# Moving the value load, cutting the filler products, and giving 345 planned steps their own due times in an attention and two-MLP kernel

## The chip, the core and the metric

One NeuronCore of a Trainium2 chip runs the kernel. The metric is the device time of one execution in microseconds (us). Engines are named as in the profile: PE is the matrix engine TensorE, DVE is VectorE, ACT is ScalarE, POOL is GpSimd, SP is the engine whose queue issues most of the DMAs. TensorE has two clock levels here, 1.2 and 2.4 GHz; a granted clock of 1.00 in the profile is the upper one.

## The reference

Attention with a mask by blocks of 64 positions, its heads joined to a matrix of 2304 tokens by 512, then two MLPs with 2048 hidden features:

```python
batch, n_heads, seq, head_dim = (4, 8, 576, 64)
scores = scale * np.matmul(q, k.transpose(0, 1, 3, 2))
scores = np.where(block_i >= block_j, scores, -1000000000.0)
attn = np.exp(scores - np.max(scores, axis=-1, keepdims=True))
attn = attn / (np.sum(attn, axis=-1, keepdims=True) + 1e-09)
x = np.matmul(attn, v)                       # to (2304, 512)
r = np.maximum(x @ w_in, 0.0)
x = (s * (r * r) + b) @ w_out                # first MLP
h = x @ w2_in
out = np.maximum(0.01 * h, h) @ w2_out       # second MLP
```

## The kernel before

The tokens are cut into five blocks (NB = 5) by position in the sequence: block k holds positions 128k to 128k+127 of all four batches, 512 tokens (the last block 256). Block 0 is the first tile. Its attention has to be finished before the first MLP can start on it. After that, the MLP of one block (16 chunks f of 128 hidden features) and the attention of the next block run side by side, so that PE always has products to do while DVE and ACT work on the softmax. The second MLP follows in six sections; it uses the seven-product scheme of Strassen and Winograd on 2 by 2 blocks.

The first tile is done in four pairs of heads (p = 0 to 3). For each pair the loads of keys (fk, L653) and queries (fq, L659) are issued, for the first three pairs half by SP and half by ACT, for the fourth all six by SP. Then come the scores (L597), the row maxima (L558), the exponentials (L567), the normalisation (L582), the transposes through PE (t, L612) with their copies out of PSUM (L528 on ACT, L530 on DVE), the product with the values (o, L700; the values of all four pairs are one load of 1 MB, fv, L666), and the split of the result into a high and a low part (xh on ACT, L708; xl on DVE, L710). Scores are laid into PSUM banks y0 to y3, outputs and every second transpose into the two banks of s.

The weights of the first MLP arrive as words of 8 bytes and are decoded chunk by chunk in block 0 (tile early): DVE shifts (L365), ACT scales (L368), DVE joins (L371), ACT takes the high part (L384), DVE takes the low part (L387). A chunk then gives the h products (m_in, L929, 12 groups of one 128x512 product), a ReLU on ACT (L945), a square on ACT or DVE (L943), a high part (L947), a low part (L948) and the y products (m_out, L972). There is one PSUM bank for h in these blocks, so the h products of a chunk wait until the ReLU and the square of the chunk before have read the bank.

To keep PE from idling ahead of that, the program issues products of a zero tile with itself (warm, L634): WARM = 8 of 128 columns and FILL = 26 of 256 columns. Each is seen as two PE instructions in the trace. The 26 have a due time of 60, later than any work of the first tile, so that the planner gives them to PE only when nothing else is ready.

The order of all instructions is made when the program is built. Graph.add collects 4516 steps, each with its engine, its estimated cost, the steps it follows, the buffers it opens and a due time. Graph.order then plays a list schedule: whenever an engine is free, it takes from the steps that are ready by the planner's clock the one with the smallest due time, and writes it next in that engine's program. On the chip each engine keeps that order, whatever the real times are. DMA steps are planned with s.wire (time on the DMA engines), s.land (time to the landing) and at most eight out at once (LANES).

Of the kernel before, what the change touches and what calls it, by code (L numbers as in the profile page):

```python
# [43 lines left out]
class Graph:  # L44
# [11 lines left out]
    def add(self, eng, fn, after=(), opens=(), uses=(), due=0.0, port=False, nbytes=0, rel=0.0, mode="f", behind=(), run=2048, tail=0.0):  # L56
# [4 lines left out]
        s.tail = tail  # L61
        s.wire = nbytes / abs(run) * (12.0 + abs(run) / 23.0) / 16e3
        s.land = 1.5 if run > 0 else 0.5
        for p in s.preds:
# [29 lines left out]
    def order(self):  # L94
# [3 lines left out]
        events, n, out_there = [], 0, 0  # L98
        port, dma, mode = None, 0.0, "f"
        out = []  # L100
        turn = {}
        for i, s in enumerate(self.steps):
            s.rank = (s.due, i)
            for b in s.opens:
                if b.key in self.inturn:
                    turn.setdefault(b.key, []).append(s)
            if not s.left:
                heapq.heappush(events, (s.rel, n, "ready", s, None))
                n += 1
        for k in turn:  # L110
            turn[k].sort(key=lambda s: s.rank, reverse=True)
        while events:
# [27 lines left out]
            for e in idle:  # L140
# [42 lines left out]
                if s.nbytes:  # L183
                    dma = max(dma, end + 1.0) + s.wire
                    end = dma + s.land
                    out_there += 1
# [18 lines left out]
def act(n, ptr=0, acc=False):  # L205
    return 0.205 + n / 1195 + 0.125 * acc


def dve(n, rate=1):
    return 0.155 + n / 960 / rate  # L210
# [8 lines left out]


NB = 5
ORDER = (0, 1, 2, 4, 3)
# [3 lines left out]
def kernel(  # L226
# [23 lines left out]
    scale = 1.0 / float(D) ** 0.5  # L250
    FILL = 26
    WARM, LATE, PACE, AHEAD = 8, 10, (6.0, 4.9), 3
# [145 lines left out]
    def first_weights():  # L398
        for f in range(NF):
# [9 lines left out]
            if f < 1:  # L409
                chunk(w, raw, f, [lds[0]], [0], due)  # L410
                a = chunk(w, raw, f, [lds[1]], [1], due + 2)
            else:
                a = chunk(w, raw, f, lds, [0, 1], due)
            if f < KEEP or f >= NF - KEEP:
                slot = f if f < KEEP else f - NF + 2 * KEEP
                kept_ok[f] = G.add(
                    {"SP": 0.65}, lambda e, w=w, slot=slot: e.dma_start(out=kept[slot], in_=w().bitcast(F32).rearrange("p a n -> p (a n)")),
                    [a], [], [w], due + 8, run=-8192, nbytes=1048576)

# [121 lines left out]
    def softmax(k, banks, cols, P, pcols, due, after):  # L541
# [11 lines left out]
        for j, bk, c, n, r in groups:  # L553
            def fn(e, j=j, bk=bk, c=c, n=n, r=r):
                i = bk()[:, c:c + n * r]
                if r > 1:
                    i = i.rearrange("p (r n) -> p r n", r=r)
                e.reduce_max(out=nm()[:, j:j + r], in_=i, axis=AX.X)  # L558
            mx.append(G.add({"DVE": dve(n * r)}, fn, [after[j + r - 1]], [nm] * (j == 0), [nm, bk], due - 4))
        neg = G.add(  # L560
# [4 lines left out]
        for j, (bk, c, n) in enumerate(cols):  # L565
            def fn(e, j=j, bk=bk, c=c, n=n):
# [3 lines left out]
                )  # L570
            ex.append(G.add({"ACT": act(n, 1, True)}, fn, [neg], [l] if j == 0 else [], [P, l, nm, bk], due - 3.5))
        a = G.add(
# [74 lines left out]
    for p in range(NP):  # L647
# [16 lines left out]
        if p == 0:  # L664
            id_ok = G.add({"SP": 0.65}, lambda e: e.dma_start(out=id_sb, in_=ident), due=-39.5, run=512, nbytes=65536)
            fv_ok = G.add({"SP": 0.65}, lambda e: e.dma_start(out=fv(), in_=v[:, :128].rearrange("b s d -> s b d")), [], [fv], due=-37.5, run=2048, nbytes=1048576)  # L666
            sb_ok = [
# [11 lines left out]
    for p in range(NP):  # L679
        due = 10.0 + 4.0 * p  # L680
        y0, y1 = [bank(key, "s") for key in (("y0", "y1"), ("y2", "y3"), ("y0", "y1"), ("y2", "y3"))[p]]
# [50 lines left out]
    def later_block(blk):  # L732
# [8 lines left out]
        for u in range(NP * B):  # L741
# [48 lines left out]
            if flat:  # L790
# [16 lines left out]
                for h in range(2):  # L807
# [5 lines left out]
                        out=P()[:, nk * h:nk * h + nk], in_=bk[h]()[:, :nk], func=ACTF.Exp, bias=nm()[:, h:h + 1], scale=1.0,  # L813
                        accum_out=l()[:, h:h + 1]), mx, [P, l] * (h == 0), [P, l, nm, bk[h]], due - 3.5)
                    for h in range(2)
# [15 lines left out]
            else:  # L831
# [6 lines left out]
                for j in range(2):  # L838
# [8 lines left out]
                    for j in range(2)  # L847
# [5 lines left out]
                        out=P()[:, half * j:half * j + half], in_=bk[j]()[:, :half], func=ACTF.Exp, bias=nm()[:, 0:1], scale=1.0,  # L853
                        accum_out=l()[:, j:j + 1]), [neg], [l] * (j == 0), [P, l, nm, bk[j]], due - 3.5)
                    for j in range(2)
# [351 lines left out]
    def out_phase(n):  # L1207
# [13 lines left out]
        for o, r in enumerate(IN_ORDER):  # L1221
            z, first = where[r]
            for i in range(4):
                due = t2[n] + 28 * ONE + (4 * o + i) * ONE if o > 1 else t2[n] + (7 * min(i + 2, 4) + 2 * (i + o / 2) + 1 * (i == 3)) * ONE
# [28 lines left out]
                after = [hi, lo, out_ok[n, r], *[ev.get(({6: 1, 7: 6, 4: 7, 3: 5}.get(r), d)) for d in range(2)]]  # L1253
                p = G.add({"PE": ONE}, fn, after, z if first and i == 0 else [], [*z, gh, gl, out_w[n, r]], due)
            for d in range(2):
# [3 lines left out]
                if fresh:  # L1259
                    a = G.add({"ACT": act(NH)}, lambda e, y=y, z=z, d=d: copy(e, y()[:, d], z[d]()[:, :NH]), [p], [y] if y.opener is None else [], [y, z[d]], due + ONE)  # L1260
                else:
                    a = G.add({"DVE": dve(NH)}, lambda e, y=y, z=z, d=d: add(e, y()[:, d], z[d]()[:, :NH]), [p, prev], [], [y, z[d]], due + ONE)
                ev[r, d] = ye[j, to[r], d] = a
# [82 lines left out]
```

## Time and profile before

| | before |
|---|---|
| time, median of 3 runs | 945.01 us (944.73 to 946.66) |
| the profiled execution's own time | 944.63 us |
| its span, first to last instruction | 942.8 us |
| PE busy | 929.3 us (99%) |
| PE weight loads busy | 828.4 us (88%) |
| DVE busy | 660.3 us (70%) |
| ACT busy | 576.8 us (61%) |
| mean granted clock of TensorE | 0.998 |

All further numbers of the kernel before are from the profiled execution. Busy time of PE counts the fillers as well as real products, and matmuls overlap a little at their ends. A time with an engine in square brackets is idle time before an instruction and the work that ended it. "us to landing" of a DMA is from its issue to the landing of its data.

### The profile page before, as it was taken

The page shows a single profiled execution, that of the slowest core. Times are in us where ns is not written, and L with a number is a line of the kernel's source. Part 1 is how long each engine was busy: PE and PEld are TensorE (multiplying, and loading weights), DVE is VectorE, ACT ScalarE, POOL GpSimd, SP SyncE. Part 2 cuts the span into 40 slices and gives each one's busy share as a digit, 9 for nine tenths or more (in the row PEclk, how much of TensorE's full clock was granted, in tenths as well). Part 3 has the DMA queues.
Part 4 walks back from the last instruction along what each step waited for, and adds up shares of the span by engine and source line. Part 5 has one row for each costly group of instructions (what it writes and reads, how often), then busy time and mean ns, then how long its engine had stood idle before and what let it go on. Part 6 is the DMA issues. An engine that isn't in the chain of part 4 may idle for free.

```text
span 942.8 us, 16507 instructions
## 1 busy us (share of the span) xinstructions
PE 929.3 (99%) x5780; PEld 828.4 (88%) x5780; DVE 660.3 (70%) x1374; ACT 576.8 (61%) x1222; POOL 26.1 (3%) x113
## 2 busy tenths in 40 slices
PE   9899999999999999999999999999999999999998
PEld 8688887777778888878888888999999999999998
DVE  5998769777787677677776745455686565855657
ACT  5888657676676665577676643464656556455543
POOL 2000000000000000000000000000000000000000
PEclk9999999999999999999999999999999999999999
DMA  8995887887858797387338983996239842157402
GB/s 235 349 312 194 277 262 267 264 275 185 253 150 271 220 286 239 123 249 227 102 95 279 369 308 105 399 417 265 101 85 339 298 172 102 51 200 275 166 1 67
DMA packets 147667, 208.26 MB, mean 221 GB/s; under 512 B 23552, under 2 KB 118400, under 8 KB 140928
## 3 DMA queue, kind: packets, MB, share of 16 engines
q1 hardware_dynamic: 145136, 206.42, 66.3%
q10 hardware_dynamic: 2448, 0.79, 0.4%
q8 instruction: 46, 0.75, 0.3%
q14 instruction: 37, 0.30, 0.1%
HBM read 154.47 MB, written 52.69 MB: 220 GB/s over the span
## 4 chain that ended last, share of the span: by engine, by line
PE 91%; DVE 4%; DMA 2%; ACT 1%; issue 1%; SPq 1%; ACTq 0%; DVEq 0%
PE y L972 21%; PE h L929 21%; PE A L1250 10%; PE A L1185 10%; PE C L1185 5%; PE C L1250 5%; PE o L880 4%; PE t L612 4%; PE B L1250 3%; PE s L802 3%; PE B L1185 2%; PE s L597 1%; PE s L841 1%; DMA fk<-in_k_dram 1%; DMA early<-in_moe_w_in_dram 1%
## 5 line engine op out<-in xcount | busy, mean ns | idle before, releaser
L929 PE MATMUL h<-xh,w 128*128 128x512 f32 (+1 forms) x640 | 209.9, 385 | 3.0 <-DVE g L943 1.9
L972 PE MATMUL y<-gh,w 128*128 128x512 f32 (+1 forms) x640 | 187.9, 377 | 0.1
L929 PEld LDWEIGHTS h<-xh,w 128*128 128x128 f32 x640 | 118.6, 189 | 29.5 <-DVE g L943 3.8
L972 PEld LDWEIGHTS y<-gh,w 128*128 128x128 f32 x640 | 112.9, 189 | 20.6 <-issue 2.4
L1243 ACT ACTIVATE gh<-G 128x384 fp32r<-128x384 f32 x168 | 87.2, 524 | 54.8 <-PE A L1250 20.3
L1057 DVE TENSOR_TENSOR gl<-G,gh 128x384 fp32r<-128x384 f32 x168 | 91.6, 555 | 41.1 <-ACT gh L1243 39.6
L929 PE MATMUL h<-xl,w 128*128 128x512 f32 (+1 forms) x320 | 118.8, 371 | 1.3 <-DVE xl L710 1.3
L972 PE MATMUL y<-gl,w 128*128 128x512 f32 (+1 forms) x320 | 118.5, 370 | 0.0
L1185 PE MATMUL A<-xh,wi 128*128 128x384 f32 x384 | 111.3, 335 | 0.0
L1250 PE MATMUL A<-gh,wo 128*128 128x384 f32 x384 | 98.0, 336 | 1.4 <-DVE Y L1165 1.4
L945 ACT ACTIVATE g<-h 128x512 f32<-128x512 f32 (+1 forms) x80 | 44.3, 553 | 60.2 <-PE h L929 53.2
L1250 PEld LDWEIGHTS A<-gh,wo 128*128 128x128 f32 x384 | 69.2, 188 | 2.3 <-DVE Y L1165 2.3
L1185 PEld LDWEIGHTS A<-xh,wi 128*128 128x128 f32 x384 | 70.6, 188 | 0.1
L972 PEld LDWEIGHTS y<-gl,w 128*128 128x128 f32 x320 | 60.3, 188 | 10.8 <-DVE gl L948 0.5
L948 DVE TENSOR_TENSOR gl<-g,gh 128x512 fp32r<-128x512 f32 (+1 forms) x80 | 50.7, 634 | 26.4 <-ACT gh L947 25.8
L929 PEld LDWEIGHTS h<-xl,w 128*128 128x128 f32 x320 | 60.8, 190 | 9.5 <-DVE xl L710 1.7
L1199 ACT ACTIVATE G<-G 128x384 f32<-128x384 f32 x72 | 37.8, 525 | 50.5 <-DVE G L1165 50.4
L612 PE MATMUL t<-id_sb,p 128*128 128x128 f32 x400 | 64.2, 275 | 2.7 <-ACT xf L528 1.0
L1185 PE MATMUL A<-xl,wi 128*128 128x384 f32 x192 | 64.4, 336 | 0.0
L1250 PE MATMUL A<-gl,wo 128*128 128x384 f32 x192 | 64.2, 334 | 0.0
L612 PEld LDWEIGHTS t<-id_sb,p 128*128 128x128 f32 x400 | 47.7, 140 | 18.0 <-issue 4.4
L1057 DVE TENSOR_TENSOR G<-G 128x384 f32<-128x384 f32 x96 | 53.3, 556 | 9.3 <-ACT G L1199 7.7
(120 smaller groups left out, 1768.1 us busy)
## 6 DMA issues: line engine op xcount, KB each, us to landing
wi<-u_in SPq DMA_DIRECT2D x32, 896.0 KB, 7.8
wo<-u_out SPq DMA_DIRECT2D x28, 1024.0 KB, 7.5
w<-kept SPq DMA_DIRECT2D x16, 1024.0 KB, 7.9
u_in<-unit SPq DMA_DIRECT2D x16, 896.0 KB, 6.2
u_out<-unit SPq DMA_DIRECT2D x32, 448.0 KB, 4.7
early<-in_moe_w_in_dram SPq DMA_DIRECT2D x16, 512.0 KB, 5.4
early<-in_moe_w_out_dram SPq DMA_DIRECT2D x16, 512.0 KB, 6.4
kept<-w SPq DMA_DIRECT2D x8, 1024.0 KB, 7.7
```

The lines of the kernel that those rows point to most:

```text
L612: e.transpose(tb()[:, x * 128:(x + 1) * 128], P()[:, pc:pc + 128], id_sb)
L802: e.matmul(out=o[h][:, :nk], lhsT=qs()[r, qc], rhs=kk()[r, :nk], start=(n == 0), stop=(n == 2))
L880: e.matmul(out=o()[64 * h:64 * h + 64, n * x:n * x + n], lhsT=V()[:, j, 64 * h:64 * h + 64], rhs=r, start=(j == 0), stop=(j == nj - 1),)
L929: e.matmul(out=h()[:, :T], lhsT=w()[:, wi, c * 128:(c + 1) * 128], rhs=x[blk, c]()[:, :T], start=(c == 0 and n == 0), stop=(c == KD - 1 an ...
L945: a = G.add({"ACT": act(T)}, lambda e: e.activation(out=g()[:, :T], in_=h()[:, :T], func=ACTF.Relu), [prev], [g], [h], due)
L948: lo = G.add({"DVE": dve(T)}, lambda e: e.tensor_tensor(out=gl()[:, :T], in0=g()[:, :T], in1=gh()[:, :T].bitcast(F32), op=ALU.subtract), [ ...
L972: e.matmul(out=y()[:, :W], lhsT=w()[:, wi, d * 128:(d + 1) * 128], rhs=x()[:, :W], start=(pos == 0 and n == 0), stop=(pos == NF - 1 and n ...
L1057: e.tensor_tensor(out=out, in0=x, in1=y, op=ALU.subtract)
L1185: e.matmul(out=x()[:, :NH], lhsT=in_w[n, i, c]()[:, s, ai], rhs=y()[:, c], start=(first and c == 0 and m == 0), stop=(c == 1 and m == 2), ...
L1199: {"ACT": act(NH)}, lambda e, y=y: e.activation(out=y(), in_=y(), func=ACTF.Prelu, alpha=0.01), [a], [], [y], d2 + 2)
L1243: hi = G.add({"ACT": act(NH)}, lambda e, gh=gh, x=x: e.activation(out=gh(), in_=x(), func=ACTF.Copy), [a], [gh], [x], due - 2)
L1250: e.matmul(out=z[d]()[:, :NH], lhsT=out_w[n, r]()[:, 2 * i + d, s], rhs=y(), start=(first and i == 0 and m == 0), stop=(i == 3 and m == 2) ...
```

## The change

Five things are changed.

1. The load of the values, fv, has a due time of -36.5 instead of -37.5. The loads of the four pairs are due at -40, -39, -38 and -37, so fv now comes after the six loads of the fourth pair in SP's queue and not before them.
2. FILL is 14 instead of 26: 22 fillers in all instead of 34.
3. The pairs of the first tile are due at 10, 11, 12 and 13 instead of 10, 14, 18 and 22.
4. A table DUE adds its own shift, in tenths of a us, to the due time of 345 of the now 4504 steps, named by their number in the order in which they are added. Counted by the line that adds them, 220 are PE steps (82 y groups, 75 h groups, 29 transposes, 26 of scores, 4 outputs of attention, 4 of the second MLP), 39 are SP's DMAs, and the rest are on DVE, ACT and POOL. The last one, 3399, lies in the first of the six sections of the second MLP. Steps 85 and 87, 116 and 118 are the second transpose and the value product of pairs 0 and 1 of the first tile; 198 and 210 are the shift of chunk 1 and the low part of chunk 2 of the weights.
5. The planner's estimates of DMAs are others (wire, land, and 0.8 instead of 1.0 from issue to start), exponentials with an accumulated sum get a tail of 0.08, and four places that named only the last of several predecessors now name them all.

```diff
+        run, into = min(abs(run), 7168), run > 0
+        s.wire = nbytes / run * (21.0 + run / 26.4 if into else 3.8 + run / 21.9) / 16e3
+        s.land = 0.82 if into else 0.33
-        s.wire = nbytes / abs(run) * (12.0 + abs(run) / 23.0) / 16e3
-        s.land = 1.5 if run > 0 else 0.5
...
+            s.due += 0.1 * DUE.get(i, 0)
...
-                    dma = max(dma, end + 1.0) + s.wire
+                    dma = max(dma, end + 0.8) + s.wire
...
+DUE = {
+    85:-261, 87:-155, 88:12, 116:-75, 118:-58, 198:-96, 203:-47, 210:-82, 211:-67, 269:-24, 270:84, 351:43, 369:-52,
...
+    3380:31, 3387:-15, 3388:-23, 3391:-29, 3399:8,
+}
...
-    FILL = 26
+    FILL = 14
...
-            mx.append(G.add({"DVE": dve(n * r)}, fn, [after[j + r - 1]], [nm] * (j == 0), [nm, bk], due - 4))
+            mx.append(G.add({"DVE": dve(n * r)}, fn, after[j:j + r], [nm] * (j == 0), [nm, bk], due - 4))
...
-            ex.append(G.add({"ACT": act(n, 1, True)}, fn, [neg], [l] if j == 0 else [], [P, l, nm, bk], due - 3.5))
+            ex.append(G.add({"ACT": act(n, 1, True)}, fn, [neg], [l] if j == 0 else [], [P, l, nm, bk], due - 3.5, tail=0.08))
...
-            fv_ok = G.add({"SP": 0.65}, lambda e: e.dma_start(out=fv(), in_=v[:, :128].rearrange("b s d -> s b d")), [], [fv], due=-37.5, run=2048, nbytes=1048576)
+            fv_ok = G.add({"SP": 0.65}, lambda e: e.dma_start(out=fv(), in_=v[:, :128].rearrange("b s d -> s b d")), [], [fv], due=-36.5, run=2048, nbytes=1048576)
...
-        due = 10.0 + 4.0 * p
+        due = 10.0 + 1.0 * p
...
-                p = G.add({"PE": ONE}, fn, after, z if first and i == 0 else [], [*z, gh, gl, out_w[n, r]], due)
+                ps.append(G.add({"PE": ONE}, fn, after, z if first and i == 0 else [], [*z, gh, gl, out_w[n, r]], due))
```

## Rows read from the trace of the kernel before

**Rows 1.** Busy by stretch: length, PE, PEld, DVE, ACT, POOL, PEclk, DMA share, GB/s

```profile
0.00:45.00 45.00, 41.17 (x271) 35.12 (x272) 32.35 (x69) 31.12 (x99) 5.52 (x21) 0.96 0.96 287
45.00:100.00 55.00, 55.00 (x310) 45.79 (x309) 48.67 (x92) 42.72 (x80) 3.71 (x16) 1.00 0.79 254
```

**Rows 2.** Groups of PE by form, the fillers of line 634: busy, mean ns, idle

```profile
L634 PE MATMUL warm<-wq 128*128 128x256 f32 x52 | 12.8, 383 | 0.0
...
L634 PE MATMUL warm<-wq 128*128 128x128 f32 x16 | 3.4, 401 | 1.3 <-POOL wq L524 1.3
```

**Rows 3.** Timeline of PE, the two waits around the first h group: start, length

```profile
36.33 0.50 PE L929 MATMUL h<-xl,w 128*128 128x512 f32 x1 [1.26 <-DVE xl L710]
...
38.87 0.79 PE L929 MATMUL h<-xh,w 128*128 128x512 f32 x1 [1.05 <-DVE g L943]
```

**Rows 4.** Busy by stretch around 40 us, columns as in rows 1

```profile
35.00:40.00 5.00, 2.70 (x10) 1.86 (x10) 4.96 (x9) 3.91 (x8) 0.31 (x1) 0.84 1.03 395
40.00:45.00 5.00, 5.00 (x22) 4.05 (x21) 4.33 (x12) 4.34 (x10) 0.15 (x1) 0.82 0.98 341
```

**Rows 5.** Chain that ended last: two h groups of 12 products, start and length

```profile
38.87 4.37 PE h L929 x12
69.84 2.76 PE h L929 x12
```

**Rows 6.** Timeline of SP's queue: issues of fv, pair 4, first weights

```profile
9.04 0.60 SPq L666 DMA_DIRECT2D fv<-in_v_dram  x1
...
12.57 1.27 SPq L659 DMA_DIRECT2D fq<-in_q_dram  x2
13.88 0.60 SPq L405 DMA_DIRECT2D early<-in_moe_w_in_dram  x1
```

**Rows 7.** Tile fq, SP's issues in 5 to 9 us, then in 10 to 14 us

```profile
L659 SPq DMA_DIRECT2D fq<-in_q_dram x4: 595/604/615, 5.3 to 8.4; - x4
...
DMA to landing us min/median/max: 3.1/3.6/3.8
...
L659 SPq DMA_DIRECT2D fq<-in_q_dram x4: 614/614/878, 10.3 to 13.2; - x4
...
DMA to landing us min/median/max: 6.0/6.3/6.4
```

**Rows 8.** Busy by stretch in the first tile, columns as in rows 1

```profile
8.00:20.00 12.00, 12.00 (x98) 11.04 (x98) 8.35 (x21) 8.00 (x45) 0.30 (x2) 1.00 1.04 254
20.00:28.00 8.00, 8.00 (x68) 6.69 (x68) 6.22 (x16) 6.97 (x29) 0.00 (x0) 1.00 1.00 361
28.00:35.00 7.00, 6.78 (x45) 5.10 (x44) 6.61 (x12) 6.41 (x9) 0.31 (x1) 1.00 1.05 306
```

**Rows 9.** Timeline of ACT, then of DVE: fourth pair and weights

```profile
24.88 0.31 ACT L567 ACTIVATE p<-s,nm 128x64 f32<-128x64 f32 x1 [0.25 <-DVE nm L561]
...
29.03 2.26 ACT L368 ACTIVATE early<-early 128x1024 f32<-128x1024 f32 x2
...
34.46 1.22 DVE L387 TENSOR_TENSOR w<-early,w 128x1024 fp32r<-128x1024 f32 x1
35.59 0.68 DVE L710 TENSOR_TENSOR xl<-o,xh 128x512 fp32r<-128x512 f32 x1
```

**Rows 10.** Waits of PE from 45 to 560 us, then to the end: us, times, longest

```profile
PE h L929 <- ACT g L945: 1.0, 1, 1.0
PE t L612 <- ACT xf L528: 1.0, 1, 1.0
PE t L612 <- DVE p L532: 0.9, 2, 0.5
PE h L929 <- DVE g L943: 0.8, 1, 0.8
PE t L612 <- ACT pv L528: 0.5, 1, 0.5
...
PE A L1250 <- DVE Y L1165: 1.4, 3, 0.5
```

**Rows 11.** Timeline of ACT: the exponentials' idle time before the third pair

```profile
17.37 0.32 ACT L567 ACTIVATE p<-s,nm 128x64 f32<-128x64 f32 x1 [1.45 <-DVE nm L561]
```

More of the change, by code (lines that the diff above doesn't have):

```diff
@@ L409, in first_weights @@
             if f < 1:
-                chunk(w, raw, f, [lds[0]], [0], due)
-                a = chunk(w, raw, f, [lds[1]], [1], due + 2)
+                a = [chunk(w, raw, f, [lds[0]], [0], due), chunk(w, raw, f, [lds[1]], [1], due + 2)]
             else:
-                a = chunk(w, raw, f, lds, [0, 1], due)
+                a = [chunk(w, raw, f, lds, [0, 1], due)]
             if f < KEEP or f >= NF - KEEP:
@@ L417, in first_weights @@
                     {"SP": 0.65}, lambda e, w=w, slot=slot: e.dma_start(out=kept[slot], in_=w().bitcast(F32).rearrange("p a n -> p (a n)")),
-                    [a], [], [w], due + 8, run=-8192, nbytes=1048576)
+                    a, [], [w], due + 8, run=-8192, nbytes=1048576)
     def walk(blk):
@@ L813, in later_block @@
                         out=P()[:, nk * h:nk * h + nk], in_=bk[h]()[:, :nk], func=ACTF.Exp, bias=nm()[:, h:h + 1], scale=1.0,
-                        accum_out=l()[:, h:h + 1]), mx, [P, l] * (h == 0), [P, l, nm, bk[h]], due - 3.5)
+                        accum_out=l()[:, h:h + 1]), mx, [P, l] * (h == 0), [P, l, nm, bk[h]], due - 3.5, tail=0.08)
                     for h in range(2)
@@ L853, in later_block @@
                         out=P()[:, half * j:half * j + half], in_=bk[j]()[:, :half], func=ACTF.Exp, bias=nm()[:, 0:1], scale=1.0,
-                        accum_out=l()[:, j:j + 1]), [neg], [l] * (j == 0), [P, l, nm, bk[j]], due - 3.5)
+                        accum_out=l()[:, j:j + 1]), [neg], [l] * (j == 0), [P, l, nm, bk[j]], due - 3.5, tail=0.08)
                     for j in range(2)
@@ L1222, in out_phase @@
             z, first = where[r]
+            ps = []
             for i in range(4):
@@ L1259, in out_phase @@
                 if fresh:
-                    a = G.add({"ACT": act(NH)}, lambda e, y=y, z=z, d=d: copy(e, y()[:, d], z[d]()[:, :NH]), [p], [y] if y.opener is None else [], [y, z[d]], due + ONE)
+                    a = G.add({"ACT": act(NH)}, lambda e, y=y, z=z, d=d: copy(e, y()[:, d], z[d]()[:, :NH]), ps, [y] if y.opener is None else [], [y, z[d]], due + ONE)
                 else:
-                    a = G.add({"DVE": dve(NH)}, lambda e, y=y, z=z, d=d: add(e, y()[:, d], z[d]()[:, :NH]), [p, prev], [], [y, z[d]], due + ONE)
+                    a = G.add({"DVE": dve(NH)}, lambda e, y=y, z=z, d=d: add(e, y()[:, d], z[d]()[:, :NH]), [*ps, prev], [], [y, z[d]], due + ONE)
                 ev[r, d] = ye[j, to[r], d] = a
```

29 rows, old and new, of the table DUE are left out of this document.

## The prediction

> **What bounds the kernel now.** I read busy time by stretch first, then the waits of PE, then the first 45 us engine by engine. From 45 to 100 us PE is busy 55.00 of 55.00 us [rows 1], and the list of PE's waits from 45 us to the end adds up to 1.0 + 1.0 + 0.9 + 0.8 + 0.5 + 1.4 = 5.6 us [rows 10]. So behind 45 us PE is the bound, its products are the same before and after, and only those 5.6 us and a little change of order can be won there. A microsecond by which the dense stretch starts earlier is a microsecond of the total.
>
> The first 45 us are different. PE counts as busy 41.17 us [rows 1], but 12.8 us of it are the 26 fillers and 3.4 us the 8 short ones [rows 2]. Two waits frame the first h group, 1.26 us for the low part of the fourth pair and 1.05 us for the square that frees the h bank [rows 3]. Right after them the granted clock is 0.84 and 0.82 in two stretches of 5 us [rows 4], that is, some of the time at 1.2 GHz, and the next h group takes 4.37 us where one at 2.4 GHz takes 2.76 [rows 5]: 1.61 us lost. What can be won in the front is therefore 12.8 + 1.26 + 1.05 + 1.61 = 16.7 us of PE time without use, as far as the work that PE waits for can be done sooner.
>
> That work is on DVE and ACT. In 8 to 35 us DVE is busy 8.35 + 6.22 + 6.61 = 21.2 of 27 us and ACT 8.00 + 6.97 + 6.41 = 21.4 [rows 8]: each has about 5.7 us of idle time, most of it ahead of 20 us, and is nearly full from 28 us on. The reason is the fourth pair: its exponentials start only at 24.88, when its maxima are there [rows 9]; the third pair's wait 1.45 us, to 17.37, for theirs [rows 11].
>
> **The change part by part.** *Values behind the fourth pair.* SP issues fv at 9.04, 1 MB, and the last two queries of the fourth pair from 12.57 [rows 6]. Queries issued before it (5.3 to 8.4) landed in 3.6 us, those behind it (10.3 to 13.2) in 6.3 [rows 7]. So the fourth pair's last load, issued at 13.2, lands at about 19.6. Without fv ahead it is issued one issue (0.60 us) earlier and lands in 3.6 to 3.8 us: about 16.3, a gain of 3.3 us for its scores. fv goes out at about 13.2, still ahead of the first weights at 13.88 [rows 6], whose queue position and bytes ahead are unchanged, so they cost nothing. The price: the values land at about 19.6 instead of 15.5, and the value product of pair 0 moves from about 17 to after 19.6. It is not the last thing that h waits for, and its followers need ACT and DVE anyway; I cost it at nothing, with an upper bound of 1.2 us, one high part and one low part pushed into the full stretch (0.68 us for the low part [rows 9], about as much for the high part).
>
> *Pairs due closer.* The maxima and exponentials of pairs 2 and 3 now go ahead of copies and value products of pairs 0 and 1. The third pair's 1.45 us wait [rows 11] should go. With scores at 16.3 to 18.3 and maxima behind them, the fourth pair's exponentials can follow the third's at about 19 to 21 instead of 24.88. The rest of the chain took 35.59 + 0.68 - 24.88 = 11.4 us [rows 9], with weight steps of 2.26 us on ACT and 1.22 on DVE set between; those came in as the larger weights had landed, and will be met less. Engine time says the same: to finish the fourth pair DVE must do what it did by 36.3 less the weights of chunk 1 and later. It can win most of its 5.7 us of idle time. I take two thirds, 3.8 us, for DVE's progress, and up to 8 us for the fourth pair's low part alone (it is then at 28 to 31, not 36.3).
>
> *Fillers.* 12 fewer are 24 instructions of 12.8/52 = 0.246 us: 5.9 us of PE time [rows 2]. This comes off the total only where the work behind them is ready 5.9 us sooner. By the last paragraph the first h group can end 6 us sooner. The second h group needs chunk 1, which was complete at 34.46 + 1.22 = 35.7 [rows 9] and used at 38.87 [rows 3]: a lead of 3.2 us. With DVE 3.8 us ahead this permits a start 3.2 + 3.8 = 7.0 us earlier. So 5.9 us fit, with idle time in their place of 0 to 3 us; I take 2.0, since the h bank's wait of 1.05 us stays and DVE has less lead to cover misses. Of the clock's 1.61 us and the wait of 1.26 us for the fourth pair, 2.87 together, I take 1.1 as won. Front: -5.9 + 2.0 - 1.1 = -5.0 us, bounds -9 (all of it, 5.9 + 1.26 + 1.61, rounded) and 0.
>
> *345 due times and the planner's DMA costs.* What they can win behind 45 us is at most the 5.6 us of waits [rows 10] and some tenths for changes between kinds of products. Nothing moves behind the first section of the second MLP, so the 1.4 us there mostly stay: at most 4.2. They also shift 157 groups of h and y products, and a group put too early stops everything behind it on PE. On SP, 39 DMAs move; a load put behind a store waits with it. The planner now reckons 0.65 + 0.8 + 0.49 + 0.82 = 2.8 us for a query load of the first tile (from the new constants; before, 0.65 + 1.0 + 0.37 + 1.5 = 3.5), where the trace has 3.1 to 3.8 [rows 7]. What is planned on a landing can thus stall about 0.8 us in its engine's order; behind the front most loads lie far ahead of use. I take -1.0 us, from +3 to -3.5. The tail of 0.08 and the fuller lists of predecessors cost nothing on PE: products of one engine end in order, so the last one's end covers the earlier ones.
>
> Sum against the profiled execution's own 944.63: -5.0 - 1.0 = -6.0 gives 938.6. That execution lies 0.38 us below the median of 945.01; on the median it is 939.0 us.
>
> **A rule that speaks against the fewer fillers.** In the trace 2.3 us of waits around a group of 12 products were followed by a stretch at 1.2 GHz [rows 3 to 5]. The Trainium skill, "TensorE: Matmul & The Clock Gate", Part 1: The HAM clock gate, says that the throttled state is the default and that activity releases it; fillers are that activity. By it the saved 5.9 us could come back as slow products: it is rival 2.
>
> **Rivals.** 1. *The fillers were only cover.* The weights' decode, not the fourth pair, sets the start: DVE is nearly full from 28 us [rows 8], so idle time replaces the 12 fillers and the second h group still starts near 38. Then only the 1.26 us wait goes and the middle decides: 943.5 to 946, say 944.5. For it: DVE's full load. Against it: 5.7 us of idle DVE ahead of 28 us. Chance 0.13.
>
> 2. *The clock halves earlier.* Idle time takes the place of the fillers in one piece, and the first two h groups run at the lower clock, at 1.61 us each [rows 5] instead of one: with the 1.1 us not won and 1.6 more lost, 939.0 + 1.1 + 1.6 = 941.7. Chance 0.15.
>
> 3. *Slower: the single h bank.* Moved h and y groups leave too little between two h groups of the first MLP, and PE stands until ReLU and square have read the bank, 0.8 to 1.05 us each time [rows 3, 10]. There are two such waits behind 45 us now; 64 chunk boundaries could have one. It decides from 6 additional waits on, which eat the 6.0 us; with 9, at 1.0 us, the time is 948. For it: 157 moved groups, placed by a planner whose loads are reckoned short. Against it: with the same planner the trace before has two. Chance 0.12.
>
> 4. *More than forecast.* Both the front's bound and the middle are won: 944.63 - 9 - 2 = 933.6, on the median 934. Chance 0.10.
>
> **How the numbers follow.** My forecast, the front shorter by 3 to 7 us and the middle about even, has 0.50 and its own range is 937 to 941.5. Rivals 2 and 4 are faster too; rival 1 is mostly within 0.2% (943.1 to 946.9), about what a measurement of this kernel can tell from no change. Faster 0.50 + 0.15 + 0.10 = 0.75, same 0.13, slower 0.12. The range from 934 to 944.8 leaves out rival 3, the upper half of rival 1 and the low edge of rival 4, about 2 in 10.
>
> **What would show it.** The fourth pair's exponentials start at 19 to 21; its queries land in under 4.5 us; fillers take about 6.9 + 3.4 us of PE; the second h group starts at 32 to 35 and no slow group of 4.4 us is left or it has moved earlier; PE's waits behind 45 us add up to 3 to 6 us. Wrong would be: the second h group at 37 or later (rival 1), a granted clock under 0.8 between 20 and 35 us (rival 2), or more than eight waits of h for g (rival 3).

## The result, and the profile after

The changed kernel takes 936.32 us (median of 4 runs, 935.63 to 937.59) beside 944.87 us for the kernel before in the same sessions: a ratio of 0.9908, 95% interval 0.9889 to 0.9926, or 8.6 us less. The profiled execution took 935.64 us, its span is 933.9 us. The forecast was 939.0 us, from 934.0 to 944.8.

In the changed file lines lie some 35 further down: h is L964, y L1007, the transposes L647, the square L978, the fillers L669. First the fillers and the stretches, columns as in [rows 2] and [rows 1]:

```profile
L669 PE MATMUL warm<-wq 128*128 128x256 f32 x28 | 6.7, 379 | 0.0
...
L669 PE MATMUL warm<-wq 128*128 128x128 f32 x16 | 3.6, 416 | 1.3 <-POOL wq L559 1.3
```

```profile
10.00:15.00 5.00, 5.00 (x37) 4.74 (x36) 2.50 (x8) 4.18 (x27) 0.00 (x0) 1.00 0.64 134
25.00:30.00 5.00, 4.54 (x30) 3.97 (x31) 5.00 (x9) 3.21 (x5) 0.00 (x0) 0.51 1.03 399
30.00:35.00 5.00, 5.00 (x33) 4.19 (x29) 3.50 (x6) 4.00 (x6) 0.00 (x0) 0.81 1.04 329
```

The fillers of 256 columns went from 12.8 to 6.7 us. The slow stretch did not go: it lies earlier and is longer, from 25.05 to 31.88 us by the trace's clock records (6.8 us; before, 38.4 to 41.8, 3.4 us), and the DMA engines, full in 10 to 15 us before (share 1.00, 274 GB/s), have a share of 0.64. The timelines of PE, SP and ACT answer to [rows 3], [rows 6] and [rows 9]:

```profile
24.86 0.30 PE L647 MATMUL t<-id_sb,p 128*128 128x128 f32 x1 [1.47 <-ACT xh L743]
...
35.68 0.50 PE L964 MATMUL h<-xh,w 128*128 128x512 f32 x1
```

```profile
12.97 0.60 SPq L701 DMA_DIRECT2D fv<-in_v_dram  x1
13.62 1.76 SPq L441 DMA_DIRECT2D early<-in_moe_w_in_dram  x1
```

```profile
19.99 0.31 ACT L602 ACTIVATE p<-s,nm 128x64 f32<-128x64 f32 x1
...
26.51 1.18 ACT L404 ACTIVATE early<-early 128x1024 f32<-128x1024 f32 x1 [1.18 <-DMA early<-in_moe_w_out_dram]
```

The fourth pair's exponentials begin at 19.99 instead of 24.88, the second h group at 35.68 instead of 38.87. The wait of 1.47 us stands in front of the transposes now, and ACT waits 1.18 us for the weights of chunk 1. Behind 45 us the waits of PE [rows 10] became, to 570 us and then to the end:

```profile
PE t L647 <- DVE pv L565: 0.9, 1, 0.9
PE t L647 <- ACT pv L563: 0.6, 2, 0.4
PE h L964 <- DVE g L978: 0.2, 1, 0.2
...
PE A L1286 <- DVE Y L1200: 1.2, 3, 0.5
PE A L1220 <- DVE G L1200: 0.2, 1, 0.2
```

That is 5.6 us before and 3.1 after. To see all of the 9.0 us of span, I split the time between the starts of neighbouring PE instructions: a real product counts with its columns at 2.4 GHz, fillers with their whole interval, idle time by itself, and what real products took beyond their columns (the lower clock, small hidden waits, change between kinds of products) once for the first 45 us and once for the rest.

| us of span | before | after | difference |
|---|---|---|---|
| columns of real products at 2.4 GHz | 811.1 | 811.1 | 0.0 |
| fillers | 14.9 | 9.5 | -5.4 |
| idle, up to 45 us (without the first 1.3) | 2.5 | 2.7 | +0.1 |
| idle, behind 45 us | 6.1 | 3.2 | -2.9 |
| beyond the columns, up to 45 us | 11.2 | 12.9 | +1.8 |
| beyond the columns, behind 45 us | 91.8 | 89.2 | -2.6 |
| ahead of the first and behind the last start | 5.3 | 5.3 | 0.0 |

Of the part up to 45 us, products that began at the lower clock have about 1.6 us before and 4.0 after. So the front gave 3.5 us (5.4 - 0.1 - 1.8); the first y group starts at 39.1 instead of 43.1. Behind it another 5.5 us were won, 2.9 of waits and 2.6 in hand-overs, time between products that no list of waits shows; the last product of the first MLP starts at 578.9 instead of 588.2.

### The profile page after: what moved, and what is told of

Its sections match the earlier page's. It is cut to its first block, busy times and chain, and to the rows that moved or that the text cites. A ratio compares the mean times of both kernels' runs of the same rounds, so it can differ in the third digit from the quotient of the medians.

```text
span 933.9 us, 16454 instructions
## 1 busy us (share of the span) xinstructions
PE 923.0 (99%) x5756; PEld 824.8 (88%) x5756; DVE 652.6 (70%) x1365; ACT 582.7 (62%) x1231; POOL 25.1 (3%) x113
## 4 chain that ended last, share of the span: by engine, by line
PE 88%; DMA 5%; DVE 2%; ACT 2%; SPq 1%; issue 1%; DVEq 0%; ACTq 0%
PE y L1007 20%; PE h L964 20%; PE A L1286 10%; PE A L1220 10%; PE C L1286 5%; PE C L1220 5%; PE t L647 4%; PE o L915 4%; PE B L1286 3%; PE s L837 2%; PE B L1220 2%; PE s L876 1%; PE s L632 1%; DMA x_dr<-xs 1%; DMA early<-in_moe_w_out_dram 1%; DMA fk<-in_k_dram 1%
## 5 line engine op out<-in xcount | busy, mean ns | idle before, releaser
L964 PE MATMUL h<-xh,w 128*128 128x512 f32 (+1 forms) x640 | 209.8, 381 | 0.3 <-DVE g L978 0.2
L1007 PE MATMUL y<-gh,w 128*128 128x512 f32 (+1 forms) x640 | 189.4, 380 | 0.0
L964 PEld LDWEIGHTS h<-xh,w 128*128 128x128 f32 x640 | 117.7, 188 | 24.3 <-issue 2.6
L1007 PEld LDWEIGHTS y<-gh,w 128*128 128x128 f32 x640 | 112.4, 189 | 21.3 <-issue 3.2
L1007 PE MATMUL y<-gl,w 128*128 128x512 f32 (+1 forms) x320 | 118.5, 370 | 0.0
L964 PE MATMUL h<-xl,w 128*128 128x512 f32 (+1 forms) x320 | 118.2, 369 | 0.0
L980 ACT ACTIVATE g<-h 128x512 f32<-128x512 f32 (+1 forms) x80 | 44.1, 551 | 43.6 <-PE h L964 38.4
L1007 PEld LDWEIGHTS y<-gl,w 128*128 128x128 f32 x320 | 60.3, 188 | 11.0 <-DVE gl L983 0.7
L647 PE MATMUL t<-id_sb,p 128*128 128x128 f32 x400 | 65.3, 279 | 3.5 <-ACT xh L743 1.5
L964 PEld LDWEIGHTS h<-xl,w 128*128 128x128 f32 x320 | 60.4, 189 | 8.1
L647 PEld LDWEIGHTS t<-id_sb,p 128*128 128x128 f32 x400 | 48.7, 142 | 17.5 <-issue 5.9
L982 ACT ACTIVATE gh<-g 128x512 fp32r<-128x512 f32 (+1 forms) x80 | 46.6, 583 | 26.4 <-PE y L1007 21.3
```

The lines of the kernel that those rows point to most:

```text
L647: e.transpose(tb()[:, x * 128:(x + 1) * 128], P()[:, pc:pc + 128], id_sb)
L964: e.matmul(out=h()[:, :T], lhsT=w()[:, wi, c * 128:(c + 1) * 128], rhs=x[blk, c]()[:, :T], start=(c == 0 and n == 0), stop=(c == KD - 1 an ...
L980: a = G.add({"ACT": act(T)}, lambda e: e.activation(out=g()[:, :T], in_=h()[:, :T], func=ACTF.Relu), [prev], [g], [h], due)
L982: hi = G.add({"ACT": act(T)}, lambda e: e.activation(out=gh()[:, :T], in_=g()[:, :T], func=ACTF.Copy), [a], [gh], [g], due)
L1007: e.matmul(out=y()[:, :W], lhsT=w()[:, wi, d * 128:(d + 1) * 128], rhs=x()[:, :W], start=(pos == 0 and n == 0), stop=(pos == NF - 1 and n ...
```

## Experiments

Two kinds of edits are used. Some change due times or counts, so that the planner makes a new order, from the first tile to the second MLP. Others take the finished order as it is and move a few steps in it; then everything else stays where it was. In those, `seq` is the list that Graph.order returns and `steps` the list of steps by number. For each run the split of the table above was made again, each from one profiled execution; "idle behind 45" below is up to 570 us (4.7 before, 1.8 after).

**1. Fewer fillers alone, planned anew.**

```diff
-    FILL = 26
+    FILL = 14
```

> The kernel before with FILL = 14 and nothing else. Theory (the fillers stand in waits that the first tile's other work sets; removing them alone gives nothing): 12 fillers, 5.4 us by the trace of the changed kernel, turn into idle time of PE, the second h group still starts at 38 to 39, the granted clock falls earlier than at 38.4; 944 to 948 us. Rival (fillers themselves hold up real products): the second h group starts 3 us or more earlier and the time is 939 to 942.

948.82 us, ratio 1.0044 (1.0028 to 1.0060), 3.7 us slower and just above the theory's range. The second h group starts later, at 40.18, behind a longer wait:

```profile
40.18 0.77 PE L929 MATMUL h<-xh,w 128*128 128x512 f32 x1 [1.50 <-DVE g L943]
```

**2. The same without a new plan: the order before, less its last 12 fillers.**

```diff
+        seq = [s for s in seq if s not in steps[27:39]]
```

> The planned order of the kernel before, kept to the letter, only without its last 12 fillers; nothing else moves, so that the middle isn't planned anew as it was with FILL = 14. Theory (the fillers only cover waits, and keep the clock up): the second h group starts at 38 to 40, PE idles 5 us more in the front, the lower clock covers more of 25 to 42 us, 945 to 947.5. Rival (they held up products): 940 to 943. Behind 45 us the waits should stay at 4.7 us up to 570 us, against 5.5 in the run with FILL = 14.

947.95 us, ratio 1.0023 (1.0012 to 1.0034). The idle time of the front is 4.5 us more (7.0), two slow stretches of 3.4 us replace one, and the second h group starts at 41.15, time and start a little beyond the theory's ranges:

```profile
PE t L612 <- ACT w L384: 3.3, 1, 3.3
PE warm L634 <- POOL wq L524: 1.3, 1, 1.3
PE h L929 <- DVE xl L710: 1.3, 1, 1.3
```

These are PE's waits in the first 45 us: 3.3 us is the place where the fillers stood. Here nothing else moved, and it shows that fillers taken off a front that isn't shorter become idle time (4.5 us for 4.4 us of fillers), with 1.8 us more beyond the columns in the front, where the second slow stretch lies. They save nothing by themselves. Run 1 shows less than that: of its 4.6 us of span 1.4 lie in the first 45 us and 3.1 behind them, in the new plan.

**3. Values behind the fourth pair and pairs closer, all fillers left.**

```diff
-            fv_ok = G.add(..., due=-37.5, ...)
+            fv_ok = G.add(..., due=-36.5, ...)
...
-        due = 10.0 + 4.0 * p
+        due = 10.0 + 1.0 * p
```

> The kernel before with the value load behind the fourth pair and pairs due at 10 to 13; still 26 fillers of 256 columns, no due times of their own. Theory (the fourth pair's chain is the cause): its exponentials start at 20 to 21, not 24.9, the second h group starts at 35 to 37, the 26 fillers are still all there, and the time is 941 to 944. Rival (the fillers set the start): the second h group stays at 38 to 39 and the time within 1 us of 945.

944.24 us, ratio 0.9986 (0.9969 to 1.0004): not told apart from no change. The fourth pair's exponentials do start at 21.00, as the theory said, but the second h group starts only 0.8 us earlier than before, where the rival had it. No slow stretch is left:

```profile
38.10 0.50 PE L929 MATMUL h<-xh,w 128*128 128x512 f32 x1 [0.75 <-ACT g L945]
```

So an earlier fourth pair with all the fillers wins little: 1.1 us of span in the front. Chunk 1's second weights land later, at 28.55 instead of 24.64; run 8 comes back to that.

**4. These two and FILL = 14.** Edits of 1 and 3 together.

> Values, pairs and FILL = 14 together on the kernel before, no due times and the old estimates of DMAs. Theory (by the two traces the front gives 5.4 us of fillers less 1.8 us of slow clock, 3.5 us, and the rest comes from the planned middle): 940.5 to 943.5, with the slow stretch between 25 and 35 us. Rival (the front gives all of it): 936 to 938.5. If DUE is needed in the front to use the room: 943.5 to 946.

949.11 us, ratio 1.0051 (1.0035 to 1.0067), slower by 4.0 us (beside 945.14 for the kernel before in the same session) and outside every expectation. Its front is shorter: 4.2 us less of fillers, 2.8 more of idle time (5.3 in all, with the clock at 1.00 throughout), the same beyond the columns, so 1.4 us less in sum. The second h group starts at 38.17, as in run 3 with all its fillers: the fillers didn't set that start. But the idle time behind 45 us is 8.4 us instead of 4.7, and products take 1.2 us more beyond their columns there.

**5. The changed kernel without the due times.**

```diff
-            s.due += 0.1 * DUE.get(i, 0)
```

> The changed kernel without its 345 due times; everything else of the change is there, the new estimates of DMAs too. Theory (front 3.5 us, the middle's 5.5 us come from the due times): 940 to 944, with 4 to 8 us of waits and slow hand-overs behind 45 us. Rival (the estimates of DMAs, not the due times, made the middle better): 936 to 939. If the new estimates alone make the middle worse: over 945.

953.06 us, ratio 1.0097 (1.0078 to 1.0116). The second h group starts earlier than in any other kernel here, at 34.73, and the kernel is slower than before by 7.9 us (945.14 in the same session), which is the last of the three outcomes expected. Lines lie one further up here. The longest of PE's waits between 45 and 570 us:

```profile
PE t L646 <- ACT pv L562: 2.9, 4, 1.9
PE h L963 <- DVE g L977: 2.3, 3, 1.7
PE o L914 <- ACT pv L562: 0.9, 1, 0.9
PE s L875 <- ACT p L886: 0.9, 2, 0.6
```

Idle behind 45 us is 9.9 us, products take 96.7 us beyond their columns there (91.8 before), and the clock fell twice in there, which the kernel before never had. In the two stretches of 4 us around these falls:

```profile
284.00:288.00 4.00, 3.82 (x12) 3.05 (x13) 3.26 (x10) 2.67 (x8) 0.51 (x2) 0.59 1.07 315
431.00:435.00 4.00, 4.00 (x35) 2.92 (x32) 1.17 (x3) 1.03 (x3) 0.00 (x0) 0.57 1.06 270
```

So, with everything else of the change in place, the 345 due times are worth 953.06 - 936.32 = 16.7 us (two sessions, in which the kernel before took 945.14 and 944.87). They first pay for a middle that the other edits made worse, then go beyond what the kernel before had. One of these other edits can be priced: runs 4 and 5 differ only in the fifth part of the change, the planner's estimates with the tail and the fuller lists of predecessors. Without due times it makes the kernel 3.9 us slower (953.06 beside 949.11 in the same session).

**6 and 7. One part of the due times alone.**

```diff
-            s.due += 0.1 * DUE.get(i, 0)
+            s.due += 0.1 * (DUE.get(i, 0) if i < 300 else 0)
```

> The changed kernel with the due times of steps below 300 alone (the first tile and the first weights, 11 of the 345). Theory (those 11 make the first 45 us as short as in the changed kernel, the other 334 are worth some 13 us behind it): the second h group within 1 us of 35.7, waits of PE from 45 to 570 us 7 us or more, 946 to 951. Rival (the 11 carry most of it): 936 to 940.

953.49 us, ratio 1.0087 (1.0061 to 1.0112), slower than either expectation; second h group at 37.75, not near 35.7, idle behind 45 us 10.6. The other part, with `i >= 300`:

> The changed kernel with the 334 due times from step 300 on alone. Theory (each due time was fitted to what stands before it, so that a first tile of another order spoils the order behind it too): the waits of PE from 45 to 570 us are back at 6 us or more and the time is 943 to 950. Rival (the 334 do their work whatever the first tile does): those waits stay under 3 us and the time is 936 to 940.

952.53 us, ratio 1.0078 (1.0050 to 1.0106), above the theory's range too; second h group at 37.60, idle behind 45 us 9.5. The longest waits there, of the first and then of the second:

```profile
PE t L647 <- ACT pv L563: 4.3, 4, 2.9
PE h L964 <- DVE g L978: 2.0, 2, 1.7
```

```profile
PE t L647 <- ACT pv L563: 3.4, 2, 2.4
PE s L876 <- ACT p L887: 1.4, 2, 1.2
```

334 due times that win 16.7 us together with 11 others win 0.5 us without them, less than the spread of those runs (951.54 to 954.24), and the 11 win nothing alone. By these two runs they fit one order, that of one front, and are no property of the steps that they name.

The span of each run beside that of the kernel before, in us, split at 45 us as above:

| run | up to 45 us | behind 45 us |
|---|---|---|
| the changed kernel | -3.5 | -5.5 |
| 1, fewer fillers, new plan | +1.4 | +3.1 |
| 2, fewer fillers, old order | +1.9 | +0.2 |
| 3, values and pairs | -1.1 | -0.1 |
| 4, front's three edits | -1.4 | +5.0 |
| 5, no due times | -2.7 | +9.9 |
| 6, early due times alone | -1.6 | +10.4 |
| 7, later due times alone | +0.6 | +6.3 |

A new plan need not be worse: run 3 was planned anew and its middle is as before.

**8. The value load back ahead of the fourth pair, the rest of the changed order untouched.**

```diff
+        seq.remove(steps[38])
+        seq.insert(seq.index(steps[53]), steps[38])
```

> The order of the changed kernel, only the load of the values put back ahead of the fourth pair's loads in SP's queue. Theory (the value load holds the fourth pair up by 3.3 us): the fourth pair's queries land at 19 to 20 instead of 16.5, its scores end at 21 to 22, the second h group starts at 38 to 39 instead of 35.7, 938.5 to 940 (936.3 + 2 to 3.5). Rival (the weights from 25 us on set the start whatever the pair does): the second h group within 1 us of 35.7 and 936 to 937.5.

935.84 us, ratio 0.9896 (0.9875 to 0.9917): not told apart from the changed kernel. The second h group starts at 36.01, near 35.7 as the rival had it. First the fourth pair's queries: SP's issue of tile fq with the times to landing, in the changed kernel (9.7 to 12.3 us), then here (10.6 to 13.2):

```profile
L694 SPq DMA_DIRECT2D fq<-in_q_dram x4: 614/614/615, 9.7 to 12.3; - x4
...
DMA to landing us min/median/max: 2.6/2.7/4.2
```

```profile
L694 SPq DMA_DIRECT2D fq<-in_q_dram x4: 614/619/623, 10.6 to 13.2; - x4
...
DMA to landing us min/median/max: 5.3/5.9/6.2
```

and, in the same way, the weights of chunk 1 in the changed kernel, then here:

```profile
L441 SPq DMA_DIRECT2D early<-in_moe_w_out_dram x1: 430/430/430, 17.5 to 17.5; - x1
...
DMA to landing us min/median/max: 8.1/8.5/8.9
```

```profile
L441 SPq DMA_DIRECT2D early<-in_moe_w_out_dram x1: 430/430/430, 19.1 to 19.1; - x1
...
DMA to landing us min/median/max: 4.7/5.1/5.4
```

The pair's last query does land 2.9 us later here (19.45 by the landing records, 16.50 in the changed kernel). But the second weights of chunk 1 land at 24.5 instead of 26.4, and ACT's wait of 1.18 us is gone. One load order buys the pair's time with the weights' time; on this front it is even.

In the changed kernel six small loads follow each other at one issue in 0.65 us and use the DMA engines to 0.64 in 10 to 15 us; with the 1 MB load among them the share is 1.00. This is not yet what delays chunk 1, since the weights of chunk 0 land at 21.94 in the changed kernel and at 21.81 here. The delay comes right behind them. In the changed kernel the DMA engines are nearly idle in 21 to 23 us, until two loads of 0.5 KB (s_sb and b_sb) have landed, at 22.77 and 23.82; here these land at 21.98 and 22.14. The changed kernel, then this run, with the columns of [rows 1]:

```profile
21.00:22.00 1.00, 0.67 (x5) 0.31 (x3) 1.00 (x3) 1.00 (x7) 0.15 (x1) 1.00 0.08 17
22.00:23.00 1.00, 0.70 (x12) 0.70 (x14) 0.92 (x3) 1.00 (x5) 0.00 (x0) 1.00 0.28 91
```

```profile
21.00:22.00 1.00, 1.00 (x17) 0.85 (x16) 0.90 (x5) 0.86 (x3) 0.00 (x0) 1.00 0.98 381
22.00:23.00 1.00, 0.83 (x9) 0.56 (x5) 1.00 (x3) 1.00 (x9) 0.07 (x1) 1.00 1.05 422
```

From chunk 0's landing to that of b_sb pass 1.6 to 2.9 us in the nine traces with the values behind the fourth pair, and 0.3 to 1.3 us in the five with the values ahead of it. Why these two small loads take longer there isn't shown.

**9. Two scalings of weights later on ACT.** In the changed kernel they stood in ACT's order ahead of the fourth pair's copies and waited for landings.

```diff
+        for i, j in ((199, 179), (207, 181)):
+            seq.remove(steps[i])
+            seq.insert(seq.index(steps[j]) + 1, steps[i])
```

> The order of the changed kernel, only two scalings of weights on ACT (line 404 at 26.5 and 29.3 us, which waited 1.18 and 0.61 us for their weights to land) put behind the two transposes' copies and the two high parts that stood behind them. Theory (ACT waits in order for a landing that the planner puts 2 us too early, and the fourth pair with it): the values' products start 1 to 2 us sooner, the second h group at 34 to 35, 934.5 to 935.8. Rival (the weights set the start): no change or up to 1 us more, 936 to 937.5.

935.57 us, ratio 0.9889 (0.9873 to 0.9906), within the noise of the changed kernel; the first h group starts 0.3 us sooner (31.50), the second 0.7 us later (36.40), not at 34 to 35. Chunk 1's second weights landed at 27.52 in this trace, 1.1 us later than in that of the changed kernel, though no load was moved.

**10. Six more fillers, to keep the clock up.**

```diff
+        for i, n in ((118, 1), (176, 3), (147, 1), (149, 1)):
+            k = seq.index(steps[i])
+            seq[k:k] = [steps[26]] * n
```

> The order of the changed kernel, with six more fillers (about 2.7 us) put before the value product of pair 1 (1), the transposes of pair 2 and 3 (3 and 1) and the value product of pair 2 (1), where PE idled 2.4 us in all. Theory (the idle time there lets the clock fall from 25.1 to 31.9, which costs 1.8 to 3.6 us): the slow stretch is gone or half as long, the second h group starts 1 us or more earlier, 934.5 to 936. Rival (the slow products there are off the chain, since ACT waits for weights to land): the clock stays up, the second h group starts within 0.5 us of 35.7, 936 to 937.

937.26 us, ratio 0.9914 (0.9897 to 0.9931). The clock stays up throughout:

```profile
25.00:30.00 5.00, 2.77 (x24) 2.27 (x25) 4.15 (x8) 2.35 (x4) 0.00 (x0) 1.00 1.03 399
30.00:35.00 5.00, 4.86 (x42) 3.79 (x39) 4.02 (x6) 4.45 (x6) 0.00 (x0) 1.00 0.97 303
```

```profile
35.91 0.50 PE L964 MATMUL h<-xh,w 128*128 128x512 f32 x1 [0.30 <-ACT g L980]
```

The second h group starts 0.2 us later than without the six. This alone doesn't say that the slow stretch was free. In this trace chunk 1's second weights landed at 27.74 instead of 26.43, though no load was moved. ACT waits for them, and PE waits 1.93 us for the copies behind them. The value products then start 1.3 us later but take 1.97 us instead of 3.68, and the first h group starts 0.4 us earlier (31.42). The value products in the changed kernel, then ACT and they in this run:

```profile
28.21 3.68 PE L735 MATMUL o<-pv,fv 128*64 128x128 f32 x32 [0.16 <-ACT pv L563]
```

```profile
27.82 1.18 ACT L404 ACTIVATE early<-early 128x1024 f32<-128x1024 f32 x1 [2.61 <-DMA early<-in_moe_w_out_dram]
...
29.52 1.97 PE L735 MATMUL o<-pv,fv 128*64 128x128 f32 x32 [1.93 <-ACT pv L563]
```

In the changed kernel ACT waits 1.00 us for those slow products, in front of the fourth pair's high part. And behind the second h group PE waits here 1.1 us for a load of keys, a wait that the changed kernel's trace doesn't have:

```profile
PE s L632 <- DMA k<-in_k_dram: 1.1, 1, 1.1
```

So six fillers keep the clock up and win nothing in sum. What the slow stretch costs by itself is not shown: the later landings stand beside it.

**11. A high part earlier.** Edit of 8, and the high part of pair 0 ahead of the first scalings on ACT.

```diff
+        seq.remove(steps[88])
+        seq.insert(seq.index(steps[186]), steps[88])
```

> The order of the changed kernel with the value load ahead of the fourth pair (as in the run before that did so, second h group at 36.0) and with the high part of pair 0 on ACT ahead of the two first scalings of weights, which it stood behind although its product had been ready 4 us. Theory (PE's longest wait in the front, 1.5 us for a bank that this high part frees, sets the start): that wait is gone or under 0.5 us, the second h group starts at 34.5 to 35.2, 934 to 935.5. Rival (the scalings, later by 0.5 us, and the weights behind them set the start): the wait is gone, the second h group within 0.5 us of 36.0, 935.5 to 937.

937.44 us, ratio 0.9920 (0.9889 to 0.9951). The wait in front of the transposes is not gone, as either expectation would have it, but got another end, 1.9 us by the profile:

```profile
PE t L647 <- ACT w L420: 1.9, 1, 1.9
```

The chain of waits puts the fourth pair's normalisation on DVE there, behind the join of the first weights; the second h group starts at 35.49.

**12. Seven steps moved, so that the pairs always go ahead of the weights.**

```diff
+        for i, j in ((88, 118), (119, 88), (186, 119), (191, 186), (187, 175), (199, 179), (207, 181)):
+            seq.remove(steps[i])
+            seq.insert(seq.index(steps[j]) + 1, steps[i])
```

> The order of the changed kernel with seven steps of the first tile moved: on ACT both high parts of pairs 0 and 1 ahead of the two first scalings of weights, and two later scalings, which waited for landings, behind the copies and high parts of pairs 2 and 3; on DVE the join of the first weights behind the fourth pair's normalisation, which it delayed by 1.1 us. Theory (the fourth pair's chain through ACT and DVE sets the first h group, and the h bank the second): the transposes of pair 2 and 3 start 1 to 1.5 us earlier than in the changed kernel (24.9), the second h group at 33.5 to 34.7 instead of 35.7, 934 to 935.5. Rival (the weights' decode sets it): the second h group within 0.5 us of 35.7 or later, 936 to 937.5.

937.03 us, ratio 0.9922 (0.9905 to 0.9939). The transposes start 0.02 us earlier than in the changed kernel and the second h group 0.65 us later:

```profile
36.33 0.50 PE L964 MATMUL h<-xh,w 128*128 128x512 f32 x1 [1.08 <-ACT g L980]
```

```profile
32.02 1.14 ACT L404 ACTIVATE early<-early 128x1024 f32<-128x1024 f32 x1
33.06 1.69 ACT L420 ACTIVATE w<-early 128x512 fp32r<-128x512 f32 x2
34.66 1.15 ACT L404 ACTIVATE early<-early 128x1024 f32<-128x1024 f32 x1
35.69 0.58 ACT L980 ACTIVATE g<-h 128x512 f32<-128x512 f32 x1
```

ACT works through without a gap from the last high part to the ReLU that frees the h bank: what was moved away from the pair stands in front of the ReLU now. In the changed kernel and in runs 8 to 12 the second h group starts between 35.49 and 36.40, whichever chain was shortened. By these traces this front is held by several chains of nearly the same length, ACT's total work among them. The landings vary as much: chunk 1's second weights land between 26.43 and 27.74 in the changed kernel and runs 9, 10 and 12, which all have one order of loads. A version that moves the ReLU ahead of the last scaling wasn't tried. None of the runs is faster than the changed kernel beyond its interval.

## Why the prediction came out right, point by point

**Direction and size.** Faster, 8.6 us where 6.0 were forecast. The sum was closer than its terms: the front was put at -5.0 and gave -3.5 in the split, the due times at -1.0, with bounds of +3 and -3.5, and 5.5 us were won behind 45 us. In the front the fillers gave 5.4 of 5.9 us, idle time cost 0.1 instead of 2.0, and where 1.1 us was booked as won from the clock and the wait, products took 1.8 us more beyond their columns. That one term came out smaller and the other larger than its bound is luck as far as the sum goes. Of the signs, the exponentials (19.99), the queries (4.2 us at most), the fillers (6.7 and 3.6 us) and the waits behind 45 us (3.1) came as said; the second h group at 35.68 missed its 32 to 35.

**What bounds it.** Right: the real products take 811.1 us in both, and the gain lies in fillers, waits and hand-overs only. The bound on the middle, "at most the 5.6 us of waits and some tenths", held in sum with 5.5 us, but for another reason: the waits gave 2.9 us, and the hand-overs, which the list of waits doesn't show, gave 2.6 where some tenths were allowed. Summing only listed waits was the weak step.

**Values behind the fourth pair.** The landing was right (16.3 forecast, 16.50 measured), and so were the exponentials (19 to 21; 19.99). The sentence that the weights "cost nothing" since their place in the queue and the bytes ahead are unchanged was wrong: chunk 0 landed as before (21.94 against 22.02), but the DMA engines were nearly idle in 21 to 23 us and chunk 1 landed later, 26.4 against 24.6 before. Run 8 shows that this edit has no net effect on the changed order.

**Fillers.** That they come off the total only where the work behind them is ready sooner was right, and run 2 shows the other case, 2.3 us slower. That the front gave 3.5 us net with 5.4 us less of fillers (5.9 forecast) belongs to the new order as a whole, the early due times included, and not to the value load: with the front's three edits alone the front is 1.4 us shorter and the kernel slower.

**The clock (rival 2).** Its sign came, a granted clock of 0.51 in 25 to 30 us, and so did the earlier slow stretch, 6.8 us long. But the slow products were transposes and value products; the clock was up again at 31.88, where the first h group starts, and no h group was slow. Its time of 941.7 did not come. Run 10 keeps the clock up and wins nothing, but its weights landed 1.3 us later, so the price of the slow stretch is open. The rule of the Trainium skill ("TensorE: Matmul & The Clock Gate", Part 1: The HAM clock gate), that activity releases the throttle, fits run 10: six fillers, and no slow stretch. Run 4 has 14 such fillers, idles 5.3 us in its front, and has no slow stretch either. The prediction's reading that 2.3 us of waits were followed by the slow stretch of the kernel before was loose: the clock fell at 38.37, within the second of the two waits.

**The due times.** The step that was mis-sized most. I priced them against the waits of the kernel before, as if the rest of the change left its middle alone. Runs 4 to 7 show that it does not: the planner lays out the 500 us behind these fronts anew, with 8 to 11 us of idle time where the kernel before has 4.7. (Run 3's plan has 4.3, so not every new front does that.) The due times win that back and more, 16.7 us against the same kernel without them.

**Rivals.** Rival 1 (fillers only cover) is what run 2 does to the kernel before, slower than it said. Rival 3 named the h bank as the place of a slower middle; in runs 5 to 7 h waits for g 1.9 to 2.3 us in all, while the transposes wait 2.9 to 4.3 us for the copies that free their bank. The missing rival was a general one: a new plan with a worse middle; runs 1, 4, 5, 6 and 7 are 3.7 to 8.7 us slower than the kernel before in the same sessions, and lose 3.1 to 10.4 us of span behind 45 us.

**What stays open.** Which of the 334 later due times carry the hand-overs' 2.6 us, and how much of the front's gain each of the 11 early ones gives, was not separated; run 7 only shows that the later ones don't work without the early ones. The new estimates of DMAs were priced on one front only, without due times (runs 4 and 5), and not under the due times. Open too are the price of the slow stretch and the reason why two small loads land so late, and the weights behind them, when the values go behind the fourth pair.

## What to carry to other kernels

In a kernel whose order is made by a list schedule, an edit near the start is two edits: its own, and a new order of everything behind it. Price the second by running the edit on the frozen order as well as planned anew, and expect fine-tuned due times to fit one order only, as they did here. Cutting fillers of the busiest engine is worth nothing where another engine's chain ends last: shorten that, then cut the fillers.

## What the runs showed that I had not expected

Taking a 1 MB load out from between small ones left the DMA engines at a share of 0.64 (134 GB/s) for 5 us, where the mix had 1.00 (274 GB/s before, and 280 in run 8). That was made good by 22 us, but then the engines had shares of 0.08 and 0.28 in two us, until two loads of 0.5 KB had landed, and the weights behind them came 1.8 us later than before although none of them had changed its place. And in the middle of the dense stretch the clock fell in run 5 after waits of PE of 0.59, 0.59 and 0.31 us, and again after waits of 1.92 and 0.78 us (0.59 and 0.57 in the two stretches of 4 us).
